# Hedgehog attention plus shifted MLP: wv loaded ahead of x tiles 2 and 3, and the later jobs in a new order

## The chip, the cores and the metric

The kernel runs on one NeuronCore of a Trainium2 chip. Its time is the device time of one execution in microseconds; the figure compared is the median of several executions. The five engines are called TensorE (PE, with its weight loads PEld), VectorE (DVE), ScalarE (ACT), GpSimd (POOL) and SyncE (SP). SP computes nothing here: it issues nearly all the DMAs, one after the other.

## The reference

Input x is 2048 tokens of 448 features (bf16). It is normalised once, and two branches and x itself are summed.

```python
xn = layernorm(x)
# A: linear attention, 16 heads of 28
q, k, v = split(xn @ wqkv)
phi(t) = concat(softmax(t @ w_phi), softmax(-(t @ w_phi)))     # per head
kv, z  = phi(k)^T v, sum of phi(k) over the tokens
A      = (phi(q) kv / (phi(q) z + 1e-6)) @ wo
# B: mixer with four groups of 112 columns, shifted by +1, -1, +2, -2 tokens
h  = gelu(layernorm(xn) @ w1);  x1 = xn + shift(h) @ w2
B  = x1 + gelu(layernorm(x1) @ w3) @ w4
out = x + A + B
```

## The kernel before

The tokens are 16 tiles of 128, called by number. The weights of q and k are multiplied into `w_phi` on the chip first (the **folds**: `wpq`, `wpk`), so that one product gives what the softmax needs. The contraction over 448 is cut into halves of 64 rows; TensorE runs a matmul of the lower 64 rows and one of the upper 64 at the same time, if they write different PSUM banks and stand next to each other in its order. There are 8 PSUM banks.

Every instruction is recorded in the order in which the code calls it, and `solve` adds the semaphore waits that the data need. Each engine then runs its own instructions in the recorded order, so **the order in the code is each engine's order**, SP's too: an instruction that waits holds all that stand behind it on its engine. A buffer or bank can only be written again when its readers are done.

The program has three parts.

1. The loads, by SP and by ScalarE's queue: x tiles 0 to 5 one by one (`load_x`), `wv` and `w1` in halves (`load_half`), the other x tiles in groups.
2. `chain([...], 600, 1)`, a list of jobs written by hand. `L` is steps of the first norm of one tile: `m` statistics (VectorE), `v` the second half of them for tile 1, whose sums ScalarE makes, `r` the power -1/2 (POOL), `a` apply on VectorE, `p` apply on POOL. `XT` transposes a normalised tile on TensorE and drains it to `xnT` by the engine named; `XD` does it with a DMA transpose on SP instead. `ZV` is V of a tile (`wv`), drained by `EV`; `ZW` a tile of the w1 product, drained through gelu by `EW`; `ZR` the rest of it; `FO` a fold, drained on VectorE; `HF` the first products of k, w2 and q. A `zip` job emits its lower halves at once and queues its upper halves, which are emitted between the lower halves of later jobs. `inside(n, job, inner)` puts `inner` behind n of the job's matmuls. `do` calls what is not TensorE's: `load_w2`, `load_w4`, `load_lap(w3)`, `load_wT` (the transposed q and k weights), `rest_T` and `h_shift` (DMAs that transpose the rest of h and shift h by tokens; both on SP), `late_3` (POOL memsets), `phi_blocks`, `kv_picks`, `kv_ones`, `spin` (matmuls without use that keep TensorE busy). `vb`, `gb`, `fb` and `wb` give the PSUM banks of `ZV`, `ZW`, `FO` and of the w2 pairs.
3. `play([...])`, the steady part, again a list in order. `k0`/`k1`, `q0`/`q1`, `w0`/`w1_` are the two halves of a pair of tiles of k, q and w2; behind k1 and q1 stand two ScalarE exponentials (`k_exp`, `q_exp`), behind `w1_` two VectorE adds. `kn` (VectorE) and `kx` (POOL) normalise phi(k); `K` adds a tile to kv; `T` is SP's DMA transpose of a q tile from `eq` to `eqT`; `lo`, `sc`, `A`, `G` are the second norm of a tile (statistics, scale, apply on VectorE if the tile is in `on_dve`, else on POOL; DMA transpose of the result); `a`/`b` the halves of a pair of w3 products, drained through gelu on ScalarE; `kc`, `kb` build the attention's kv blocks; `N` is the attention of a tile; `f` 1 to 4 the last products of a pair of tiles (w4 and wo); `S` stores a tile; `wo_in` loads `wo` into `wv`.

`q_exp` of tiles i and i+1 writes slots i % 8 and i % 8 + 1 of `eq`, which has eight slots:

```python
R.act(eq[:, i % 8:i % 8 + 2, s, :, 0:DH], two(2 * b)[:, :, 0:D]...)   # q_exp
R.dma_t(eqT(i), eq_rows[:, i % 8, :])                                  # T
```

Lines in the profile: matmuls are L204, TensorE transposes L208, ScalarE's activations L212, most of VectorE and POOL L216, DMA transposes L219, other DMAs L222. Tile names are those of the memory region: `banks` is PSUM, `hi` holds `eq` and the transposed weights, `phik` later holds gelu(w3), `vaug` later the attention's and the output's buffers, `w` stands for w1, w2, w3 and w4.

## Time and profile before

| | us |
|---|---|
| median of 3 runs | 174.32 (174.0 to 176.05) |
| the profiled execution's own time | 174.06 |
| its span | 172.3 |
| TensorE matmul busy | 166.9 (97%) |
| VectorE busy | 110.9 (64%) |
| POOL busy | 90.0 (52%) |
| ScalarE busy | 82.0 (48%) |

The span goes from the first to the last instruction of the program; the time of the execution is 1.8 us longer. All times of views are counted from the span's start. A busy TensorE is one with a matmul in flight; as matmuls overlap, short waits between them don't show as idle. SP and the queues of other engines (SPq, ACTq) are shown by what they issue; the time from the start of an issue to the landing of the data is a column of its own.

### The profile page before, as it was taken

To read this page: it belongs to the slowest core of one execution; us is meant where nothing else is said; L and a number is where in the kernel's file an instruction comes from. 1 tells how busy PE (TensorE), PEld (TensorE's weight loads), DVE (VectorE), ACT (ScalarE), POOL (GpSimd) and SP (SyncE) were. 2 spreads that over 40 slices of the span, in tenths; PEclk is the share of its full clock that TensorE was granted. 3 is DMA by queue.
4 is the path that set the end of the run, shared out by engine and by line. 5 is a ranking of instruction groups with operands and counts; after the bars stand their busy time and mean duration, and the time that the engine had idled before them with its cause. 6 is when DMAs were issued, how large, how long until landed. Compare 5 with 4: busy or idle time off the path is not lost.

```text
span 172.3 us, 5315 instructions
## 1 busy us (share of the span) xinstructions
PE 166.9 (97%) x2308; PEld 96.6 (56%) x2308; DVE 110.9 (64%) x251; ACT 82.0 (48%) x107; POOL 90.0 (52%) x121
## 2 busy tenths in 40 slices
PE   7799999999999999999999999999999999999994
PEld 7545888874555555554544554554545545555563
DVE  3799943749999989918955873525817416474621
ACT  4478876777987899646133322133133212044000
POOL 5456970004779999860574289332441522724540
PEclk9999999999999999999999999999999999999999
DMA  5995546499998955161057557554961120233331
GB/s 127 330 248 92 104 67 158 87 352 220 334 159 174 135 124 138 21 76 30 11 114 97 111 105 146 94 103 106 136 135 34 30 57 4 57 34 84 88 87 50
DMA packets 51111, 20.07 MB, mean 116 GB/s; under 512 B 42256, under 2 KB 50384, under 8 KB 51088
## 3 DMA queue, kind: packets, MB, share of 16 engines
q1 hardware_dynamic: 49968, 18.86, 56.0%
q10 hardware_dynamic: 1120, 0.87, 1.6%
q8 instruction: 18, 0.29, 0.8%
q14 instruction: 5, 0.04, 0.1%
HBM read 7.14 MB, written 1.84 MB: 52 GB/s over the span
## 4 chain that ended last, share of the span: by engine, by line
PE 92%; DMA 3%; ACT 1%; DVE 1%; issue 0%; ACTq 0%
PE banks L204 91%; DMA wv<-in_A_wqkv_dram 3%; PE banks L208 1%; ACT xnT L212 1%; DVE wpq L216 1%; ACT vaug L212 0%; ACTq L222 0%; ACT L366 0%; DVE vaug L216 0%
## 5 line engine op out<-in xcount | busy, mean ns | idle before, releaser
L212 ACT ACTIVATE phik<-banks 128x1024 bf16<-128x1024 f32 (+1 forms) x44 | 42.2, 986 | 63.6 <-PE banks L204 63.4
L204 PE MATMUL banks<-gT,w 64*128 64x512 bf16 x392 | 49.2, 376 | 0.1
L216 DVE TENSOR_TENSOR vaug<-banks,vaug 128x464 f32<-128x464 f32 (+3 forms) x65 | 32.8, 513 | 20.6 <-PE banks L204 18.9
L204 PE MATMUL banks<-w,phik 64*128 64x448 bf16 (+3 forms) x434 | 45.2, 343 | 0.0
L216 POOL TENSOR_TENSOR xnT<-vaug 128x196 bf16<-128x196 f32 (+1 forms) x32 | 18.1, 587 | 47.8 <-DVE vaug L216 47.8
L204 PE MATMUL banks<-wv,xnT 64*128 64x448 bf16 (+3 forms) x222 | 32.8, 346 | 1.4 <-DMA wv<-in_A_wqkv_dram 1.2
L204 PEld LDWEIGHTS banks<-w,phik 64*128 64x128 bf16 (+1 forms) x434 | 22.9, 94 | 19.4 <-issue 0.4
L722 POOL TENSOR_TENSOR phik<-phik,rks 128x1792 bf16<-128x1792 bf16 x8 | 25.6, 3214 | 10.7 <-DVE rks L216 10.5
L204 PEld LDWEIGHTS banks<-gT,w 64*128 64x128 bf16 x392 | 18.0, 94 | 18.7 <-PE banks L204 1.1
L204 PEld LDWEIGHTS banks<-wv,xnT 64*128 64x128 bf16 (+1 forms) x222 | 13.8, 94 | 10.0 <-ACT xnT L212 1.6
L216 POOL TENSOR_TENSOR vaug<-xn,xtok 128x448 f32<-128x448 bf16 x16 | 16.2, 1033 | 0.2 <-DVE vaug L216 0.2
L216 DVE TENSOR_REDUCE ksum<-phik 128x64 f32<-128x1792 bf16 x8 | 16.0, 1994 | 0.0
L216 POOL TENSOR_TENSOR rs<-mv,mhalf 128x1 f32<-128x1 f32 (+2 forms) x18 | 12.4, 694 | 6.6 <-DVE mv L216 6.6
L204 PE MATMUL banks<-xnT,w 64*128 64x512 bf16 x84 | 15.7, 377 | 0.0
L216 DVE RECIPROCAL vaug<-banks 128x16 f32<-128x16 f32 x16 | 4.0, 252 | 17.4 <-PE banks L204 17.4
L204 PE MATMUL banks<-wpk,xnT 64*128 64x448 bf16 x112 | 14.9, 350 | 0.1
L212 ACT ACTIVATE hi<-banks 128x896 bf16<-128x896 f32 x16 | 13.8, 931 | 1.0 <-PE banks L204 1.0
L204 PE MATMUL banks<-wpq,xnT 64*128 64x448 bf16 x112 | 14.2, 349 | 0.0
L204 PE MATMUL banks<-w,hT 64*128 64x448 bf16 x96 | 12.9, 349 | 0.0
L216 DVE TENSOR_TENSOR xn<-banks,xn 128x512 bf16<-128x512 f32 (+1 forms) x16 | 9.0, 606 | 3.0 <-PE banks L204 2.9
L216 DVE BATCH_NORM_STATS2 st<-xn 128x6 f32<-128x448 bf16 x16 | 9.4, 589 | 0.0
L216 DVE BATCH_NORM_STATS2 st<-xtok 128x6 f32<-128x448 bf16 x15 | 9.1, 606 | 0.0
(72 smaller groups left out, 165.4 us busy)
## 6 DMA issues: line engine op xcount, KB each, us to landing
w<-in_B_w_dram SPq DMA_DIRECT2D x2, 896.0 KB, 5.7
out_dram<-vaug SPq DMA_DIRECT2D x15, 112.0 KB, 2.0
w<-in_B_w_dram SPq DMA_DIRECT2D x1, 1568.0 KB, 10.0
xtok<-in_A_x_dram SPq DMA_DIRECT2D x2, 448.0 KB, 7.4
wv<-in_A_wo_dram SPq DMA_DIRECT2D x2, 224.0 KB, 2.9
xtok<-in_A_x_dram SPq DMA_DIRECT2D x3, 112.0 KB, 2.6
xtok<-in_A_x_dram ACTq DMA_DIRECT2D x3, 112.0 KB, 2.8
w<-in_B_w_dram SPq DMA_DIRECT2D x1, 336.0 KB, 4.3
```

The lines of the kernel that those rows point to most:

```text
L204: self.op("PE", lambda e: e.matmul(out, lhsT, rhs, start=start, stop=stop, skip_group_check=True), [out], [lhsT, rhs], tile=self._tile(lhsT))
L208: self.op("PE", lambda e: e.transpose(out, in_, ident), [out], [in_, ident], tile=self._tile(in_))
L212: self.op("ACT", lambda e: e.activation(out, in_, func, **kw), [out], [in_] + aps)
L216: self.op(eng, lambda e: getattr(e, name)(out, *args, **kw), [out], aps)
L722: R.op(pool, lambda e: e.tensor_tensor(ph, ph, wide, op=ALU.mult), [ph], [ph, wide, *after])
```

## The change

`wv` is issued second on both queues, ahead of x tiles 2 and 3, and the halves of `wv` and `w1` trade queues. The first norm's steps are put in an order in which tiles 2 and 3 come after tile 1's sums and the spins ahead of the first transpose; one power instruction still serves tiles 1 and 2. All later jobs of the chain stand in a new order, with other banks and in part other engines for the drains. The DMAs that the chain issues move with it: `load_w2` comes ahead of the DMA transposes of tiles 8, 11 and 9 (it came behind), `load_w4` ahead of `w3`, `rest_T(1)` and `h_shift(1)` (it came last). In the play list the same 258 jobs stand in a new order; among them T goes 0, 2, 3, 5, 1, 4, 7, 6, 8, 12, 10, 11, 9, 14, 13, 15, and nine tiles instead of five have their second norm applied on VectorE. The number of instructions is the same but for the drains and applies that change engine.

```diff
         R.op("ACT", lambda e: e.preload_act_table_set("gelu_apprx_tanh_and_others"), [], [])
         load_x(0, 1)
         load_x(1, 1, "ACT")
+        load_half(wv, wv_d, 0)
+        load_half(wv, wv_d, 1, "ACT")
         load_x(2, 1)
         load_x(3, 1, "ACT")
-        load_half(wv, wv_d, 1)
-        load_half(wv, wv_d, 0, "ACT")
         load_x(4, 1)
         load_x(5, 1, "ACT")
-        load_half(w1, B_w1, 1)
-        load_half(w1, B_w1, 0, "ACT")
+        load_half(w1, B_w1, 0)
+        load_half(w1, B_w1, 1, "ACT")
         load_x(6, 2)
         load_x(8, 4)
         load_x(12, 4)
...
-        fb = {(1, 0): 2, (1, 2): 2, (0, 0): 2, (0, 2): 5}
+        fb = {(1, 0): 1, (1, 2): 6, (0, 0): 0, (0, 2): 5}
...
-        wb = {0: 3, 2: 2, 4: 2, 6: 0, 8: 0, 10: 0, 12: 2, 14: 2}
+        wb = {0: 1, 2: 2, 4: 2, 6: 0, 8: 0, 10: 0, 12: 2, 14: 2}
...
-        vb = {0: 7, 1: 6, 2: 0, 3: 2, 4: 4, 5: 5, 6: 1, 7: 0, 8: 4, 9: 5, 10: 0, 11: 6, 12: 3, 13: 2, 14: 0, 15: 1}
-        gb = ((5, 2, 3), (7, 6, 5), (4, 1, 0), (7, 7, 4))
+        vb = {0: 5, 1: 4, 2: 1, 3: 2, 4: 4, 5: 5, 6: 2, 7: 1, 8: 3, 9: 6, 10: 4, 11: 3, 12: 7, 13: 0, 14: 4, 15: 7}
+        gb = ((7, 2, 3), (6, 7, 0), (5, 3, 0), (2, 1, 4))
-            L(("m", 0), ("m", 2), ("r", 0, 1), ("a", 0), ("m", 3), ("v", 1), ("r", 1, 2), ("a", 2), ("a", 1), ("r", 3, 1)),
-            XT(0, 2, 1, "ACT"), do(spin, 5, 256), L(("a", 3), ("m", 4), ("m", 5), ("r", 4, 1), ("r", 5, 1)),
-            inside(1, ZV(0, EV(0, "ACT", 1)), XT(2, 5, 1, "ACT")), XT(3, 3, 1, "ACT"), ZV(2, EV(2, "ACT", 1)),
-            inside(1, ZV(3, EV(3, "ACT", 1)), XT(1, 3, 1, "ACT")), ZV(1, EV(1, "ACT", 1)), L(("a", 4), ("m", 7)),
-            ZW(0, 0, EW(0, 0, 1)), L(("a", 5)), XT(5, 0, 1, "ACT"),
-            L(("m", 6), ("m", 9), ("r", 7, 1), ("m", 8), ("r", 6, 1), ("r", 8, 1), ("a", 7), ("a", 6), ("m", 10)), ZW(0, 2),
-            L(("m", 11), ("a", 8)), XD(8), L(("m", 12)), XT(4, 0, 1, "ACT"), L(("r", 9, 1)), ZW(0, 1, EW(0, 1, 2)), L(("a", 9)),
-            ZV(4, EV(4, "ACT", 1)), XD(9), XT(7, 0, 1, "ACT"), L(("r", 10, 2), ("a", 10)), XT(6, 6, 1, "ACT"), L(("m", 13)),
-            ZV(5, EV(5, "ACT", 1)), do(phi_blocks), ZV(7, EV(7, "DVE", 1)), ZW(1, 1, EW(1, 1, 1)), ZV(6, EV(6, "ACT", 1)),
-            L(("p", 11), ("r", 12, 1), ("m", 15)), inside(2, ZW(1, 0, EW(1, 0, 1)), XT(10, 2, 1, "ACT")), L(("r", 13, 1)),
-            ZW(1, 2, EW(1, 2, 1)), L(("p", 12), ("r", 15, 1)), inside(3, ZV(8, EV(8, "ACT", 1)), FO(1, 0, 0)), L(("m", 14)),
-            XD(11), L(("r", 14, 1)), do(load_wT, 0, (1, 2, 3)), L(("a", 13)), inside(1, ZV(10, EV(10, "ACT", 1)), FO(1, 0, 1)),
-            L(("a", 15)), ZR(0, 7, (rest_out, 0, 7), (rest_T, 0), (h_shift, 0)), ZV(9, EV(9, "DVE", 1)), XT(12, 3, 1, "ACT"),
-            L(("p", 14)), do(load_w2), XT(13, 1, 1, "ACT"), ZV(11, EV(11, "ACT", 1)), ZW(2, 2, EW(2, 2, 1)), do(late_3),
-            XT(14, 2, 2, "DVE"), ZW(2, 0, EW(2, 0, 1)), ZW(2, 1, EW(2, 1, 1)), do(load_lap, w3, B_w3), FO(1, 2, 0),
-            inside(3, ZW(3, 0, EW(3, 0, 1)), FO(1, 2, 1)), ZR(1, 6, (rest_out, 1, 6)),
-            inside(3, ZW(3, 2, EW(3, 2, 1)), FO(0, 0, 0)), ZV(15, EV(15, "ACT", 1)), do(kv_ones),
-            inside(3, ZW(3, 1, EW(3, 1, 1)), FO(0, 0, 1)), do(rest_T, 1), inside(1, ZV(14, EV(14, "ACT", 1)), FO(0, 2, 0)),
-            FO(0, 2, 1), ZV(13, EV(13, "ACT", 1)), ZV(12, EV(12, "DVE", 1)), HF(0, 0), do(kv_picks), HF(1, 0), HF(2, 0), HF(0, 1),
-            do(h_shift, 1), HF(1, 1), do(load_w4), HF(2, 1)], 600, 1)
-
-        on_dve = (4, 6, 7, 9, 12)
+            L(("m", 0), ("r", 0, 1), ("a", 0)), do(spin, 5, 256), XT(0, 2, 1, "ACT"),
+            L(("v", 1), ("m", 2), ("m", 3), ("r", 1, 2), ("a", 2)), ZV(0, EV(0, "ACT", 1)),
+            L(("a", 1), ("r", 3, 1), ("a", 3), ("m", 4)), XT(2, 0, 1, "ACT"), L(("r", 4, 1)), XT(3, 2, 1, "ACT"),
+            L(("m", 5), ("m", 6), ("p", 4), ("r", 5, 1), ("r", 6, 1), ("m", 7)), XT(1, 6, 1, "ACT"), L(("m", 8)),
+            ZV(2, EV(2, "ACT", 1)), do(load_w2), ZV(3, EV(3, "ACT", 1)), L(("a", 5)), ZV(1, EV(1, "ACT", 1)), L(("r", 8, 1)),
+            ZW(0, 0, EW(0, 0, 1)), XT(4, 0, 1, "ACT"), L(("r", 7, 1), ("m", 11), ("a", 6), ("p", 8)), ZW(0, 2),
+            inside(1, ZW(0, 1, EW(0, 1, 2)), XT(5, 5, 1, "ACT")), ZV(4, EV(4, "ACT", 1)),
+            L(("a", 7), ("m", 10), ("m", 13), ("r", 10, 2), ("m", 9), ("p", 11)), XT(7, 0, 1, "ACT"),
+            L(("m", 15), ("r", 9, 1)), XT(6, 6, 1, "ACT"), L(("r", 15, 1)), ZV(5, EV(5, "ACT", 1)), ZV(7, EV(7, "DVE", 1)),
+            L(("a", 10), ("m", 12)), ZW(1, 1, EW(1, 1, 1)), L(("a", 9)), ZV(6, EV(6, "ACT", 1)),
+            inside(2, ZW(1, 2, EW(1, 2, 1)), XT(10, 4, 1, "DVE")), L(("r", 13, 1)), ZW(1, 0, EW(1, 0, 1)), XD(8), XD(11),
+            ZV(8, EV(8, "ACT", 1)), XD(9), do(phi_blocks), FO(1, 0, 0), ZV(10, EV(10, "ACT", 1)), L(("m", 14), ("a", 15)),
+            inside(1, ZR(0, 7, (rest_out, 0, 7), (rest_T, 0), (h_shift, 0)), FO(1, 0, 1)),
+            L(("r", 14, 1), ("r", 12, 1), ("a", 14), ("a", 12)), do(load_wT, 0, (1, 2, 3)), ZV(9, EV(9, "ACT", 1)),
+            ZV(11, EV(11, "DVE", 1)), L(("p", 13)), XT(12, 4, 1, "ACT"), XT(14, 1, 2, "DVE"), ZW(2, 2, EW(2, 2, 1)),
+            inside(3, ZW(2, 0, EW(2, 0, 1)), FO(1, 2, 0)), XT(13, 1, 1, "DVE"), FO(1, 2, 1), do(load_w4),
+            ZW(2, 1, EW(2, 1, 1)), ZW(3, 2, EW(3, 2, 1)), do(late_3), inside(2, ZW(3, 0, EW(3, 0, 1)), FO(0, 0, 0)),
+            FO(0, 0, 1), FO(0, 2, 0), ZV(15, EV(15, "DVE", 1)), ZR(1, 3, (rest_out, 1, 3)), do(load_lap, w3, B_w3),
+            ZV(14, EV(14, "DVE", 1)), ZW(3, 1, EW(3, 1, 1)), HF(1, 0), ZV(13, EV(13, "DVE", 1)), FO(0, 2, 1),
+            ZV(12, EV(12, "DVE", 1)), HF(0, 0), do(rest_T, 1), HF(1, 1), do(kv_picks), HF(2, 0), HF(0, 1), do(kv_ones),
+            do(h_shift, 1), HF(2, 1)], 600, 2)
+
+        on_dve = (3, 4, 5, 10, 11, 12, 13, 14, 15)
...
-            (T, 0), (T, 1), (k0, 1), (w0, 2), (kn, 0), (k1, 1), (w1_, 2), (lo, 0), (q0, 1), (k0, 2), (kx, 0), (k1, 2), (kn, 1), (w0, 4),
-            (kx, 1), (q1, 1), (T, 2), (T, 3), (q0, 2), (lo, 1), (w1_, 4), (kn, 2), (q1, 2), (T, 4), (T, 5), (lo, 3), (k0, 3), (K, 0), (k1, 3), (kn, 3),
-            (kx, 2), (lo, 2), (kx, 3), (q0, 3), (sc, 0), (K, 1), (q1, 3), (T, 6), (T, 7), (A, 1), (A, 0), (k0, 4), (G, 0), (A, 3), (w0, 6),
-            (A, 2), (K, 2), (k1, 4), (G, 1), (G, 2), (K, 3), (G, 3), (q0, 4), (w1_, 6), (q1, 4), (k0, 5), (K, 4), (kn, 4),
-            (w0, 8), (k1, 5), (q0, 5), (kx, 4), (K, 5), (lo, 4), (w1_, 8), (kn, 5), (q1, 5), (K, 6), (k0, 6), (w0, 10),
-            (k1, 6), (kx, 5), (q0, 6), (w1_, 10), (lo, 5), (q1, 6), (k0, 7), (K, 7), (kn, 6), (k1, 7), (q0, 7), (lo, 6),
-            (K, 8), (q1, 7), (lo, 7), (w0, 12), (kn, 7), (wo_in,), (kx, 6), (a, 0), (sc, 4), (w1_, 12), (b, 0), (A, 4),
-            (G, 4), (A, 6), (K, 9), (A, 5), (G, 5), (G, 6), (a, 1), (K, 10), (A, 7), (K, 11), (b, 1), (a, 2), (K, 12),
-            (b, 2), (kx, 7), (a, 3), (w0, 14), (a, 4), (G, 7), (lo, 9), (b, 3), (K, 13), (b, 4), (K, 14), (K, 15), (a, 5),
...
+            (q0, 1), (k0, 1), (T, 0), (w0, 2), (k1, 1), (lo, 1), (lo, 0), (kn, 0), (kx, 0), (w1_, 2), (q1, 1), (k0, 2),
+            (q0, 2), (k1, 2), (w0, 4), (T, 2), (lo, 3), (T, 3), (kn, 1), (q1, 2), (T, 5), (w1_, 4), (K, 0), (lo, 2), (k0, 3),
+            (kx, 1), (T, 1), (K, 1), (k1, 3), (T, 4), (kn, 2), (q0, 3), (sc, 0), (k0, 4), (q1, 3), (K, 3), (w0, 6), (kn, 3),
+            (k1, 4), (kx, 2), (kx, 3), (w1_, 6), (q0, 4), (kn, 4), (T, 7), (wo_in,), (K, 2), (A, 3), (T, 6), (q1, 4),
+            (k0, 5), (A, 2), (w0, 8), (A, 0), (k1, 5), (q0, 5), (w1_, 8), (lo, 5), (q1, 5), (K, 4), (G, 2), (A, 1), (kn, 5),
+            (k0, 6), (kx, 4), (w0, 10), (k1, 6), (q0, 6), (w1_, 10), (lo, 6), (lo, 4), (G, 1), (kx, 5), (lo, 7), (q1, 6),
+            (K, 5), (G, 0), (T, 8), (K, 6), (k0, 7), (sc, 4), (q0, 7), (k1, 7), (K, 8), (G, 3), (w0, 12), (q1, 7), (kn, 6),
+            (w1_, 12), (A, 4), (lo, 11), (A, 5), (a, 0), (lo, 9), (K, 10), (kn, 7), (K, 7), (b, 0), (lo, 10), (K, 11),
+            (G, 5), (a, 1), (w0, 14), (a, 2), (kx, 6), (A, 7), (b, 1), (b, 2), (K, 12), (A, 6), (w1_, 14), (a, 3), (G, 4),
...
```

## The prediction

> **What bounds the kernel now.** I read the page's busy shares, then its chain, then busy time by stage, the timeline of TensorE at the head, and last the timeline of SP's queue, which the change rearranges most.
>
> ```profile
> PE 166.9 (97%) x2308; PEld 96.6 (56%) x2308; DVE 110.9 (64%) x251; ACT 82.0 (48%) x107; POOL 90.0 (52%) x121
> PE banks L204 91%; DMA wv<-in_A_wqkv_dram 3%; PE banks L208 1%; ACT xnT L212 1%; DVE wpq L216 1%; ACT vaug L212 0%; ACTq L222 0%; ACT L366 0%; DVE vaug L216 0%
> ```
>
> TensorE is the chain: 91% of the span is one matmul after another, and one DMA (`wv`) is the only other link above 1%. Columns of the next view: stretch, then busy time and instructions of each engine, clock, DMA share, GB/s.
>
> ```profile
> 5.43:7.57 2.14, 0.94 (x14) 0.61 (x14) 1.28 (x5) 0.60 (x1) 1.23 (x2) 1.00 1.05 345
> 7.57:12.40 4.83, 4.65 (x67) 2.63 (x68) 4.66 (x14) 3.33 (x7) 2.41 (x4) 1.00 1.20 296
> 12.40:37.30 24.90, 24.81 (x448) 19.49 (x446) 15.35 (x41) 18.55 (x32) 10.17 (x17) 1.00 0.63 126
> 37.30:66.20 28.90, 28.80 (x423) 15.47 (x420) 27.89 (x39) 25.05 (x31) 22.84 (x12) 1.00 1.06 197
> 66.20:170.00 103.80, 103.52 (x1330) 54.39 (x1326) 58.81 (x149) 31.58 (x33) 50.40 (x66) 1.00 0.41 79
> ```
>
> From 12.4 us on TensorE is never idle for long; from 37.3 to 66.2 us VectorE is just as full (27.89 of 28.90) and the DMA engines are full too (1.06). A busy TensorE hides waits, so I went through the starts of its matmuls: a pair of half-height 448-column matmuls takes 0.187 us, and every larger distance is a stall. After 13 us these add up to only 1.9 us; 0.75 us of them lie after 56 us. So a new order of the later jobs can win 1.9 us at the very most, and lose without limit. What else can be won lies ahead of 13 us.
>
> **The head.** The next rows are TensorE's, from its timeline.
>
> ```profile
> 5.43 0.29 PE L208 MATMUL banks<-ident,xn 64*128 64x64 bf16 x8
> 5.65 0.72 PE L204 MATMUL banks<-gT 128*128 128x256 bf16 x5
> 7.57 0.35 PE L204 MATMUL banks<-wv,xnT 64*128 64x448 bf16 x1 [1.20 <-DMA wv<-in_A_wqkv_dram]
> 10.62 0.74 PE L204 MATMUL banks<-wv,xnT 64*128 64x448 bf16 x6 [0.17 <-ACT xnT L212]
> ```
>
> Tile 0 is transposed at 5.43, and then TensorE waits for `wv` until 7.57. The landings, issue plus time to landing: x2 3.86, x3 4.05, `wv` 6.47 (SP) and 7.43 (ACT), x4 7.62, x5 8.06. The change lets `wv` trade places with x2 and x3. The same bytes go through the same queues, so what is ahead of x4 ends when it did. `wv` took 2.6 us behind its predecessor on SP and 3.4 us on ACT; behind x0 (3.25) and x1 (3.42) it lands at 5.85 and 6.8, a gain of 0.6 us. x2 then takes the time that x4 took behind `wv` (1.15 us on SP, 0.6 on ACT): 7.0 and 7.4, a loss of 3.1 to 3.4 us. Bounds for x2: 6.45 (0.6 us behind `wv`) and 7.6.
>
> VectorE follows by its rows: statistics 0.62 + 0.20, step 0.77; apply 0.41; POOL's power 0.6. Tile 2's statistics 7.05-7.85, then tile 3's until 8.6 (they stand ahead of the apply), apply of 2 to 9.0, of 1 to 9.4, of 3 to 9.8. Tile 1 waits too: its power is now one instruction with tile 2's. Before, all four were normalised by 8.09. TensorE does tile 0's transposes (five spins now ahead of them, +0.5), four `wv` matmuls, and is idle until 9.0; the transposes of tiles 2, 3, 1 end at 10.4. By 10.4 us the kernel before has issued 17 `wv` matmuls and 32 transposes, 2.0 us of work; the new one 4 and 32, 0.8 us. It is **1.2 us behind**. From there it has all it needs, while the old one loses another 0.5 us until 14 us; so 0.7 us behind at 15 us (bounds 0 and 1.5, the two landings of x2 and whether ScalarE, 3.3 of 4 us busy here, keeps up).
>
> **From 15 to 37 us.** Per job nothing is added: the same 16 V products, 12 w1 tiles, folds and 13 TensorE transposes. Drains move from ScalarE to VectorE (V of tiles 11, 13, 14, 15; transposes of 10 and 13: 0.62 or 0.37 us each), which has room (15.35 of 24.90). On SP the three `w2` loads (24.39 to 26.95 before) now stand ahead of the transposes of tiles 8, 11, 9. SP issued without a pause from 7.5 to 34 us, so these three go from 15.65 to about 17.4, and the last, which also needs tile 9's apply at about 20.5, lands at 23.5 where V of tile 9 is due at 23: 0 to 1 us. The fold drain ahead of the first k product keeps about its 0.3 us stall. Bank by bank the new numbers leave each drain (0.54 to 1.09 us) at least one job, so I take the banks at nothing (bounds -0.6, all this stage's stalls, and +1). Together the delay at 37 us is 0.5 to 1.5 us.
>
> **The transposes of eq, which I think decide.** SP's queue:
>
> ```profile
> 28.31 4.55 SPq L222 DMA_DIRECT2D hT<-hT  x6
> 32.90 1.14 SPq L222 DMA_DIRECT2D w<-in_B_w_dram  x2
> 34.08 1.29 SPq L219 DMA_TRANSPOSE hRT<-gT  x1
> 35.41 3.85 SPq L222 DMA_DIRECT2D hT<-hT  x6
> 39.30 0.59 SPq L222 DMA_DIRECT2D w<-in_B_w_dram  x1
> 40.02 18.45 SPq L219 DMA_TRANSPOSE eqT_lo<-hi  x8
> ```
>
> The loads are w3 (32.90) and w4 (39.30). The first transpose T(0) spent 6.74 us in its issue, until 46.76, w4's last bytes; the first lands at 50.16, the second, T(1), at 53.33, the fifth at 56.21. `eq` has eight slots: q_exp of pair 4 writes slots 0 and 1 and must wait for T(0) and T(1).
>
> ```profile
> 53.62 1.73 ACT L212 ACTIVATE hi<-banks 128x896 bf16<-128x896 f32 x2 [0.39 <-PE banks L204]
> ```
>
> That is this q_exp, released by TensorE: T(1) was done 0.3 us earlier. The new order makes T(1) the fifth (T 0, 2, 3, 5, 1), and puts w4 and w3 both ahead of the shift of h, which is ahead of T(0). Work on SP ahead of w4 is what was ahead of w3, so w4 issues at about 33; its bytes (5.3 us before, 42 to 47.3) go from 35 to 40.3, w3's (34 to 39.5) to 45.6, rest and shift (2.6 us) to 48. T(0) leaves its issue at 47.3, half a us later than before, and by the old cadence the fifth lands 9.4 us later: 56.7. q_exp takes 1.75: 58.5. The next q product of pair 5, (q0, 5), uses the banks that it drains. Summed by their rows (0.755 for the first half of a k, q or w pair, 0.567 for the second, 0.226 for a KV tile) the play list has 17.5 us of TensorE work ahead of (q0, 5); the old kernel had done that much at 55.7. So it resumes **2.8 us late**. Behind the q_exp on ScalarE stand k_exp 5 and q_exp 5, whose banks are wanted 2.1 us after. This delay is against the clock, not added to the head's: the later of the two holds, and the 0.7 us is swallowed. Bounds: T(1) at 54.3 (behind 48, five transposes of 1.0 us without pauses and 1.3 to land) gives 0.6, at 58.7 gives 4.8.
>
> The Trainium skill ("DMA: Bandwidth & Descriptors", section "Queues, rings and completion order") says that an engine's descriptors are consumed in ring order; by this rule alone, bytes in order and nothing else, T(1) would land at 54.3 and the sum be 175.0. T(0)'s 6.74 us issue agrees with the order, but the gaps of 1 to 3 us between later landings are more than bytes.
>
> **After 56 us.** The wait gives VectorE and POOL 2 us to catch up, so close margins (K 14 behind the eighth k product, the first w3 products behind the fourth g transpose, both within 0.5 us by the sums) hold. Four more g_apply on VectorE (0.41 against 0.76 on POOL) lie where VectorE is half idle. The same 0.75 us of stalls: 0 (bounds -0.7 and +1).
>
> **Sum.** The profiled execution took 174.06 (span 172.3 and 1.8 around it), 0.3 below the median of 174.32. 174.06 + 2.8 + 0 = **176.9 us**.
>
> **Rivals.** (1) *T(1) in time*: transposes without pauses, 54.3; then the head's 0.7 us and 0.2 for tile 9 remain, 175.0. For it: DMA engines can move a 256 KB transpose in 1 us (49 to 51 us, 246 GB/s). Against: 135 and 24 GB/s at 47-49 and 51-53, behind the same w4. (2) *The other side: faster.* `wv` at 5.85 frees TensorE, and x2 lands with it: it needs tile 2 applied by 7.5, that is x2 by about 5.9, then the 0.6 us of the wait and half of the stalls until 13 us go, and T(1) has to be in time: -1.2 us, 172.9. For it: the DMA engines were nearly empty from 3.5 to 4.75 us, and a shorter first queue might fill this. Against: in the old order nothing behind `wv` landed before 7.6. That the change doesn't do what it says, `wv` still at 7.4, would be rival 1 or the forecast plus nothing, as T(1) holds anyway. (3) *SP held by the norms*: the transposes of 8, 11, 9 wait for POOL's and VectorE's applies with everything behind them; if w4 leaves at 35 instead of 33, T(1) lands at 58.7, +4.8: 178.9, and the first w3 products wait for the fourth g transpose.
>
> **Numbers.** Forecast 0.46 (own range 175.7 to 178.0), rival 1 0.17, rival 2 0.14, rival 3 0.23. The range 173.0 to 179.8 leaves out half of rival 2 and a quarter of rival 3. Over 2% (3.5 us, about what a measurement of this kernel can tell from no change; its runs went from 174.0 to 176.05) means below 170.8 or above 177.8. Above: most of rival 3 and an eighth of the forecast, 0.28; below: 0.03; within: 0.69.
>
> **What would show it.** Right: `wv` landing near 5.9 and 6.8, x2 near 7.0; TensorE idle from 7.6 to 9.0; T(1) landing at 56 to 57.5; ScalarE's q_exp of pair 4 released by a DMA, and TensorE idle for over 1.5 us near 56. Wrong: T(1) landing before 54; x2 before 6; a stall of over 1 us anywhere after 60, or SP waiting for a norm by over 1 us.

## The result, and the profile after

The changed kernel took **176.45 us** (median of 16 executions, 175.59 to 177.88) where the kernel before took 174.05 (16 executions on the same chip, 173.8 to 176.05): ratio 1.0136, 95% interval 1.011 to 1.0161. The forecast was 176.9. A ratio, here and below, leaves out the executions that fell in the chip's slower state, so it need not be the quotient of two medians. The profiled execution of after took 176.26 (span 174.5), that of before 174.06: 2.2 us to explain.

The page of after, its engines and the second line of its chain:

```profile
PE 165.7 (95%) x2308; PEld 99.9 (57%) x2308; DVE 118.8 (68%) x259; ACT 79.2 (45%) x102; POOL 87.7 (50%) x119
PE banks L204 68%; DVE st L216 5%; DVE ksum L216 3%; DVE xn L216 3%; DMA xnT<-xn 2%; DMA eqT_lo<-hi 2%; DMA xtok<-in_A_x_dram 2%; POOL phik L722 2%; DVE mv L216 2%; DVE g_tok L216 2%; POOL rs L216 1%; ACT hi L212 1%; ACT phik L212 1%; DVE rks L216 1%; DVE vaug L216 1%
```

TensorE's matmuls are 68% of the chain instead of 91%. VectorE, two DMA transposes and a product of POOL (`phik`, L722) are links now, none of them a large one: the loss is in several places. The same stretches of time as before (columns: stretch, then busy time and instructions of PE, PEld, DVE, ACT, POOL, clock, DMA share, GB/s):

```profile
5.43:7.57 2.14, 1.15 (x12) 0.39 (x12) 1.78 (x5) 0.60 (x1) 0.99 (x2) 1.00 1.04 349
7.57:12.40 4.83, 4.27 (x67) 2.52 (x69) 4.66 (x15) 3.68 (x7) 3.10 (x7) 1.00 1.15 259
12.40:37.30 24.90, 23.03 (x430) 17.51 (x428) 19.32 (x40) 14.88 (x26) 10.49 (x18) 1.00 0.75 134
37.30:66.20 28.90, 28.62 (x410) 17.25 (x407) 28.11 (x47) 24.14 (x29) 21.88 (x11) 1.00 1.00 203
66.20:170.00 103.80, 102.39 (x1334) 56.46 (x1331) 62.22 (x147) 32.96 (x35) 48.29 (x63) 1.00 0.41 72
```

From 12.4 to 37.3 us TensorE is idle for 1.9 us where it was for 0.1, and after 66.2 us for 1.4 instead of 0.3. VectorE carries 4 us more from 12.4 to 37.3 and 3.4 more behind 66.2. A second measure says when this shows: add up the columns of all matmuls but the spins in the order of the program, and ask how much later after reaches the sum that before has reached.

| time in before, us | 13.8 | 19.0 | 22.2 | 34.0 | 46.8 | 54.9 | 57.0 | 67.4 | 75.5 | 77.5 | 92.5 | 168.5 |
|---|---|---|---|---|---|---|---|---|---|---|---|---|
| after is later by, us | -0.69 | -0.66 | +1.63 | +1.24 | +0.67 | +1.00 | +1.23 | +1.75 | +1.64 | +2.84 | +2.18 | +2.26 |

The head gains 0.7; 2.3 us are lost at 19 to 22 us; 1 us comes back until 47 us, of which 0.7 are stalls that only the old list has (at 31.0, 38.0 and 41.7 us); then 0.2 us are lost at 56, 0.5 at 67 and 1.2 at 78 us; and some 0.5 come back, for two stalls of the old list at 79.6 and 86.1. The timeline of TensorE in after has a row behind each wait, with the releaser in brackets:

```profile
6.34 0.93 PE L204 MATMUL banks<-wv,xnT 64*128 64x448 bf16 x4 [0.69 <-ACT xnT L212]
7.77 0.29 PE L208 MATMUL banks<-ident,xn 64*128 64x64 bf16 x8 [0.50 <-DVE xn L216]
8.42 0.41 PE L208 MATMUL banks<-ident,xn 64*128 64x64 bf16 x16 [0.36 <-DVE xn L216]
...
23.41 0.54 PE L204 MATMUL banks<-wv,xnT 64*128 64x448 bf16 x3 [1.63 <-DMA xnT<-xn]
...
56.92 0.55 PE L204 MATMUL banks<-wpq,xnT 64*128 64x448 bf16 x4 [0.27 <-ACT hi L212]
...
68.25 1.04 PE L204 MATMUL banks<-gT,w 64*128 64x512 bf16 x8 [0.41 <-DMA gT<-g_tok]
...
79.67 0.63 PE L204 MATMUL banks<-vaug,phik 64*128 64x59 bf16 x32 [1.00 <-POOL phik L722]
```

These are V of tile 9 (its DMA transpose landed at 23.27), the first half of q of pair 5, the first w3 product (the fourth g transpose landed at 67.90) and K 14. By the distances of the starts they cost 1.79, 0.43, 0.54 and 1.16 us; V of tile 8 costs another 0.41 at 18.4.

SP's queue in after, the rows behind these (start and time in issue):

```profile
14.42 1.85 SPq L222 DMA_DIRECT2D w<-in_B_w_dram  x3
16.31 4.03 SPq L219 DMA_TRANSPOSE xnT<-xn  x3
...
31.57 3.10 SPq L222 DMA_DIRECT2D w<-in_B_w_dram  x3
34.71 1.98 SPq L219 DMA_TRANSPOSE hRT<-gT  x1
36.74 3.76 SPq L222 DMA_DIRECT2D hT<-hT  x6
41.63 14.02 SPq L219 DMA_TRANSPOSE eqT_lo<-hi  x7
```

w2 at 14.42 stands ahead of the transposes of tiles 8, 11 and 9, as the diff says. T(0) issues at 41.63 and is out of its issue after 1.89 us; the fifth, T(1), landed at 55.04. The q_exp of pair 4 on ScalarE is released by it:

```profile
55.14 1.73 ACT L212 ACTIVATE hi<-banks 128x896 bf16<-128x896 f32 x2 [0.94 <-DMA eqT_lo<-hi]
```

**A long instruction on POOL holds the apply on VectorE.** This was nowhere in the prediction. VectorE in after:

```profile
21.92 2.60 DVE L216 TENSOR_SCALAR xn<-xtok,mv,rs 128x512 bf16<-128x512 bf16 x2
...
69.49 2.52 DVE L216 TENSOR_SCALAR g_tok<-xn,mv,rs 128x512 bf16<-128x512 bf16 x1
...
72.70 0.37 DVE L216 TENSOR_SCALAR g_tok<-xn,mv,rs 128x512 bf16<-128x512 bf16 x1
```

and POOL in after:

```profile
22.57 1.81 POOL L434 MEMSET phik<- 128x2048 bf16 x1 [0.20 <-DVE xn L216]
...
68.65 3.21 POOL L722 TENSOR_TENSOR phik<-phik,rks 128x1792 bf16<-128x1792 bf16 x1 [0.47 <-DVE rks L216]
71.85 1.69 POOL L216 TENSOR_SCALAR g_tok<-xn,rs 128x512 bf16<-128x512 bf16 x2
76.40 3.21 POOL L722 TENSOR_TENSOR phik<-phik,rks 128x1792 bf16<-128x1792 bf16 x1 [2.85 <-DVE rks L216]
```

The same apply takes 0.37 us at 72.70 and 2.52 at 69.49. The long one ends at 72.01, 0.15 us behind POOL's product (71.86); the pair at 21.92, tiles 14 and 12, ends at 24.52, 0.14 behind the memset (24.38). The memset is released by tile 14's apply, so it starts just in time to hold tile 12's. The long apply at 69.49, tile 4's second norm, stands ahead of the eighth k norm on VectorE; that ends at 76.3, the eighth k product on POOL at 79.6, and K 14 waits for it.

So there are three suspects to be parted: w2 ahead of the transposes, T(1) as the fifth, and the applies beside POOL. The head, which came out with the other sign, is a fourth question.

### The profile page after: what moved, and what is told of

It reads as the page before. It is cut to its first block, busy times and chain, and to the rows that moved or that the text cites. A ratio compares the mean times of both kernels' runs of the same rounds, so it can differ in the third digit from the quotient of the medians.

```text
span 174.5 us, 5320 instructions
## 1 busy us (share of the span) xinstructions
PE 165.7 (95%) x2308; PEld 99.9 (57%) x2308; DVE 118.8 (68%) x259; ACT 79.2 (45%) x102; POOL 87.7 (50%) x119
## 4 chain that ended last, share of the span: by engine, by line
PE 68%; DVE 16%; DMA 7%; POOL 3%; ACT 2%; issue 1%; SPq 1%; ACTq 0%
PE banks L204 68%; DVE st L216 5%; DVE ksum L216 3%; DVE xn L216 3%; DMA xnT<-xn 2%; DMA eqT_lo<-hi 2%; DMA xtok<-in_A_x_dram 2%; POOL phik L722 2%; DVE mv L216 2%; DVE g_tok L216 2%; POOL rs L216 1%; ACT hi L212 1%; ACT phik L212 1%; DVE rks L216 1%; DVE vaug L216 1%
## 5 line engine op out<-in xcount | busy, mean ns | idle before, releaser
L204 PE MATMUL banks<-gT,w 64*128 64x512 bf16 x392 | 48.5, 376 | 0.4 <-DMA gT<-g_tok 0.4
L204 PEld LDWEIGHTS banks<-w,phik 64*128 64x128 bf16 (+1 forms) x434 | 24.1, 94 | 18.1 <-issue 0.4
L722 POOL TENSOR_TENSOR phik<-phik,rks 128x1792 bf16<-128x1792 bf16 x8 | 25.6, 3214 | 13.2 <-DVE rks L216 13.2
L204 PEld LDWEIGHTS banks<-gT,w 64*128 64x128 bf16 x392 | 19.5, 94 | 17.6 <-ACT phik L212 1.6
L212 ACT ACTIVATE hi<-banks 128x896 bf16<-128x896 f32 x16 | 13.8, 922 | 2.0 <-PE banks L204 1.1
L204 PE MATMUL banks<-w,hT 64*128 64x448 bf16 x96 | 13.4, 349 | 0.0
L212 ACT ACTIVATE hT<-banks 128x512 bf16<-128x512 f32 (+1 forms) x11 | 7.0, 638 | 4.5 <-PE banks L204 4.4
```

The source lines that it names most:

```text
L204: self.op("PE", lambda e: e.matmul(out, lhsT, rhs, start=start, stop=stop, skip_group_check=True), [out], [lhsT, rhs], tile=self._tile(lhsT))
L212: self.op("ACT", lambda e: e.activation(out, in_, func, **kw), [out], [in_] + aps)
L722: R.op(pool, lambda e: e.tensor_tensor(ph, ph, wide, op=ALU.mult), [ph], [ph, wide, *after])
```

## The experiments

Each time is a median, each ratio is to the kernel before on the same chip, with its 95% interval. Most of these intervals overlap with each other and with that of after (1.011 to 1.0161), so what one edit does is read in the traces; by their times alone only `order_4` and `order_5` are told from after.

**1. w2 behind the transposes** (`w2_late`).

```diff
-            ZV(2, EV(2, "ACT", 1)), do(load_w2), ZV(3, EV(3, "ACT", 1)), ...
+            ZV(2, EV(2, "ACT", 1)), ZV(3, EV(3, "ACT", 1)), ...
-            XT(12, 4, 1, "ACT"), XT(14, 1, 2, "DVE"), ...
+            XT(12, 4, 1, "ACT"), do(load_w2), XT(14, 1, 2, "DVE"), ...
```

> Theory: the w2 loads ahead of them make the DMA transposes of tiles 8, 11 and 9 late; with w2 behind them they issue some 1.9 us sooner, tile 9's lands near 21.4 instead of 23.3, and the stalls of TensorE at 18.4 (0.4 us) and 21.6 us (1.8 us) go. But T(1) still lands near 55.0, so the stall ahead of (q0, 5) grows from 0.4 to about 1.5 us and the time falls by 0.3 us only: 176.1. Rival A: the stalls add up, the 2.2 us come off the end: 174.3. Rival B: the transposes are late through something else (the norms of tile 9, slow packets at 20 to 21.5 us): the stall at 21.6 stays over 1 us, 176.4.

177.53 us, ratio 1.0189 (1.0128 to 1.0249): none of the three numbers. The transposes of tiles 8 and 9 landed at 17.16 and 20.88 (19.00 and 23.27 in after), both stalls were gone, and TensorE was 0.37 us ahead of the kernel before at 22 us: rival B falls. Then it lost more than it had won, in two new places, on its timeline:

```profile
24.41 0.52 PE L208 MATMUL banks<-ident,xn 64*128 64x64 bf16 x24 [1.52 <-DVE xn L216]
...
33.60 0.35 PE L204 MATMUL banks<-w,hT 64*128 64x448 bf16 x1 [1.22 <-DMA w<-in_B_w_dram]
```

The first is tile 12's apply, 2.64 us for the pair with tile 14: a wait that lay hidden behind the late transpose in after. The second is w2 itself, landed at 34.98: the new list uses it at 32 us. That is what the early w2 buys.

**2. The apply of tile 4 moved** (`a4_first`).

```diff
-... (q1, 7), (kn, 6), (w1_, 12), (A, 4), (lo, 11), (A, 5), ...
+... (q1, 7), (A, 4), (kn, 6), (w1_, 12), (lo, 11), (A, 5), ...
```

> Only (A, 4) is moved, ahead of (kn, 6) on VectorE, where no product of POOL runs beside it. Theory: its 2.52 us (0.41 elsewhere) are a wait for POOL's k product that runs beside it; moved, it takes about 0.4 us, the eighth k norm ends some 1.7 us sooner, the eighth k product ends before 78 us instead of 79.6, and the 1.2 us stall ahead of K 14 goes: 175.3. Rival: VectorE has too much ahead of the eighth k norm in any case (statistics of 11 and 9, A 5), or A(4) is slow wherever it stands: the stall stays at 0.8 us or more, 176.2 to 176.5.

177.72 us, 1.0206 (1.0142 to 1.027). VectorE:

```profile
21.98 3.78 DVE L216 TENSOR_SCALAR xn<-xtok,mv,rs 128x512 bf16<-128x512 bf16 x2
...
69.29 0.41 DVE L216 TENSOR_SCALAR g_tok<-xn,mv,rs 128x512 bf16<-128x512 bf16 x1 [2.26 <-POOL rs L216]
...
73.90 1.76 DVE L216 TENSOR_SCALAR g_tok<-xn,mv,rs 128x512 bf16<-128x512 bf16 x1
```

and POOL:

```profile
72.30 3.21 POOL L722 TENSOR_TENSOR phik<-phik,rks 128x1792 bf16<-128x1792 bf16 x1 [3.05 <-DVE rks L216]
```

Tile 4's apply takes 0.41 us where nothing of POOL runs beside it, as the theory says. Now the next one, tile 5's, lies beside the seventh product and takes 1.76; it ends at 75.66, 0.15 behind the product (75.51). The time still went up: VectorE waited 2.26 us for the scale (`sc`, POOL) in front of the moved apply, the seventh and eighth k norms were later by that, a w2 product waited 1.1 us at 72 us for VectorE's adds, and the stall ahead of K 14 grew to 1.78 us. The pair at 21.98 took 3.78 us: three memsets of POOL follow each other there until 25.61, and the second apply ends at 25.76.

**3. The old order of the loads** (`old_loads`).

```diff
-        load_half(wv, wv_d, 0)
-        load_half(wv, wv_d, 1, "ACT")
         load_x(2, 1)
         load_x(3, 1, "ACT")
+        load_half(wv, wv_d, 1)
+        load_half(wv, wv_d, 0, "ACT")
         load_x(4, 1)
```

> The changed kernel with x2 and x3 loaded ahead of wv again, its jobs as they are. Theory (from the two traces): the load order is what gains 0.65 us at 13 to 18 us, so this kernel waits for wv until about 7.5 us and is 0.5 to 1 us behind the changed kernel at 15 us; as T(1) decides at 56 us by the clock, at most 0.3 us of it are left at the end: 176.4 to 176.7. Rival A (the prediction's working): x2 early is worth more than wv early, this kernel is 0.5 us or more ahead at 15 us, 175.8 to 176.4. Rival B: the gain is the jobs' order and not the loads': no difference at 15 us.

177.94 us, 1.0216 (1.0148 to 1.0284). At 15 us it was 0.61 us ahead of the kernel before, just as after: rival B. The two executions aren't quite alike, since TensorE's clock came up at 3.95 us in after and at 5.63 here (see the last section); but `order_2`, with the new loads and the clock up at 5.88, was 0.5 us ahead, so the new load order gains nothing that these traces show. `wv` landed at 6.58 and 6.73, x2 at 3.97; in after `wv` at 4.63 and 4.82, x2 at 5.60. Either way tile 0's first product starts only when ScalarE has drained its transposes. Everything else on SP came about 0.6 us later (the first x in one piece of two tiles 9.21 against 8.61), and the transpose of tile 8 landed at 20.63, for a stall of 2.05 us. That the load order made it late isn't shown: in `kv_8` below, with the loads of after and the issue at 16.31 as in after, it landed at 20.24.

**4. The old play list behind the new chain** (`old_list`): `play([...])` and `on_dve` of the kernel before, all else as changed.

> The changed kernel up to the first q product (loads, norms, V, w1, folds), with the old list of later jobs and the old set of g_apply on VectorE. Theory: the new list costs 1.4 us (from +0.8 at 40 us to +2.2 at the end), and the old one with w4 and w3 early would have T(1) second and land it by 52: 174.9, with TensorE some 0.8 us behind the kernel before at 40 us and 0.5 to 0.9 at the end. Rival: the 0.8 us at 40 us are caught up by stalls that the old list has anyway (0.75 us): 174.2. Rival: the old list with the new SP order has a stall of its own: 176 or more.

176.07 us, 1.0109 (1.0075 to 1.0143). T(1), second here, landed at 50.49, and no matmul waits for it. TensorE is 1.9 us behind at 24 us and 2.0 at the end. That is the last rival's number, but hardly its reason: the one stall of the old list that is longer behind the new chain takes 0.65 us at 39.6 instead of 0.2 at 38.0. So in these executions the chain alone costs nearly all of it, and behind it the new list ends little later than the old one: the lag of 0.8 us that I took as the chain's at 40 us was small only because the new list has fewer stalls between 31 and 42 us.

**5. w2 where it lands in time, and the memset behind tile 12** (`order_2`), **and with T(1) second** (`order_2t`).

```diff
-    R.op(pool, lambda e: e.memset(pad, 0.0), [pad], [xn[:, NT - 2, :]])
+    R.op(pool, lambda e: e.memset(pad, 0.0), [pad], [xn[:, NT - 4, :]])
-            ZV(2, EV(2, "ACT", 1)), do(load_w2), ZV(3, ...
+            ZV(2, EV(2, "ACT", 1)), ZV(3, ...
-            ... do(load_wT, 0, (1, 2, 3)), ZV(9, EV(9, "ACT", 1)),
+            ... do(load_wT, 0, (1, 2, 3)), do(load_w2), ZV(9, EV(9, "ACT", 1)),
```

> Two edits: w2 behind the last weight transposes (issued near 23 us, so that it lands well ahead of its first use at 31 us), and POOL's memset of phik's pad waits for tile 12's apply (the last on VectorE) instead of tile 14's. Theory: VectorE's two applies near 21.9 us take 0.7 us together instead of 2.6 (and 3.8 in a4_first), since no memset of POOL runs beside the second; the transposes of tiles 8 and 9 land by 17.2 and 21; so the stalls at 18.4, 21.6 and 22.5 to 24.8 us all go, and TensorE is within 0.3 us of the kernel before at 30 us. From there: T(1) lands as in all runs of this list at 55.0 to 56.0, so TensorE waits 1.3 to 2.3 us ahead of (q0, 5) and the end stays near 176.0 to 176.6 (the two delays are not added). Rival A: they are added; T(1) comes in time, 174.2 to 174.8. Rival B: the long applies have nothing to do with the memset: 2.6 us again and a stall of over 1 us at 22 to 25 us.

> order_2, and T(1) second instead of fifth. Theory: T(1) lands near 50.5, as in old_list, nothing waits ahead of (q0, 5), and the gain of order_2 reaches 66 us: TensorE within 0.5 us of the kernel before there; left are 0.4 us at 67 and 1.2 us at 78 us (K 14), less the 0.7 us that the kernel before loses at 79 to 86: 174.6. Rival: T(1) was not what held order_2, no difference from it.

`order_2`: 177.39 us, 1.0165 (1.0097 to 1.0233). `order_2t`: 176.59, 1.012 (1.0075 to 1.0165). The two applies took 1.11 and 0.73 us together instead of 2.60: rival B falls, it is the memset. VectorE of `order_2`:

```profile
21.65 1.11 DVE L216 TENSOR_SCALAR xn<-xtok,mv,rs 128x512 bf16<-128x512 bf16 x2
```

Its second apply still waits for an apply on POOL, which ends at 22.61, 0.14 us ahead of it. The stall at 24 us was gone in both. But w2 now stood ahead of the shift of h on SP, whose last part landed at 35.34 and 34.65 (33.37 in after) and held the first w2 product for 1.3 and 0.9 us; and SP had to wait for the norms of tiles 11 and 9 (0.8 and 0.4 us), a wait that w2 had filled. Tile 9's transpose, issued at 18.34 and 18.40, landed at 22.62 in `order_2`, for a stall of 1.3 us, and at 20.79 in `order_2t`, for none. What T(1) does is seen in the two timelines of TensorE, `order_2` first:

```profile
58.65 0.55 PE L204 MATMUL banks<-wpq,xnT 64*128 64x448 bf16 x4 [0.89 <-ACT hi L212]
```

```profile
56.91 0.92 PE L204 MATMUL banks<-wpq,xnT 64*128 64x448 bf16 x8
```

A wait of 1.05 us by the starts with T(1) fifth (it landed at 56.77, so rival A falls too), none with T(1) second. `order_2t` was 1.0 us behind at 15 us in its profiled execution, of which more below.

**6. The eighth k norm and product first** (`kv_8`).

```diff
-        on_dve = (3, 4, 5, 10, 11, 12, 13, 14, 15)
+        on_dve = (3, 10, 11, 12, 13, 14, 15)
-            (w1_, 12), (A, 4), (lo, 11), (A, 5), (a, 0), (lo, 9), (K, 10), (kn, 7), (K, 7), ...
+            (w1_, 12), (kn, 7), (lo, 11), (a, 0), (lo, 9), (K, 10), (K, 7), ...
-            ... (kx, 6), (A, 7), (b, 1), ... (kx, 7), (a, 4), ...
+            ... (kx, 6), (kx, 7), (A, 5), (A, 4), (A, 7), (b, 1), ... (a, 4), ...
```

> The changed kernel with the eighth k norm right behind the seventh on VectorE, the eighth k product right behind the seventh on POOL, and the g_apply of 4 and 5 on POOL behind both. Theory: nothing of VectorE stands beside a product that it would have to wait for; the eighth k norm ends by 72.5 instead of 76.3, the eighth product by 76 instead of 79.6, and the stall of 1.2 us ahead of K 14 goes: 1.1 us faster than the changed kernel on the same chip. Rival: POOL has no room for the two g_apply (0.78 us each), and the w3 products of the second group wait for its g transposes near 88 us by 1 us or more: no gain.

176.39 us, 1.0125 (1.0069 to 1.0181); the interval is too wide for a difference of 1 us from after. In the trace the eighth norm ended at 73.0, the eighth product at 76.32, and K 14 waited for nothing. 0.73 us were lost again at 86 us, where the w3 products of the second group waited for their last g transpose (86.79), behind T(12) on SP: the theory, with a part of the rival.

**7. All of these** (`order_3`), with the fourth g transpose ahead of T(8); and **the same with w2 put between** the transposes of tile 8 and of tiles 9 and 11, and the last g transposes of the second group moved up (`order_4`).

```diff
-            ... ZW(1, 0, EW(1, 0, 1)), XD(8), XD(11), ZV(8, EV(8, "ACT", 1)), XD(9), do(phi_blocks), ...
+            ... ZW(1, 0, EW(1, 0, 1)), XD(8), do(load_w2), XD(9), XD(11), ZV(8, EV(8, "ACT", 1)), do(phi_blocks), ...
-            ... (a, 3), (G, 5), (G, 4), ... (K, 9), (G, 7), ... (G, 6), (a, 5), ...
+            ... (a, 3), (G, 5), (G, 4), (G, 7), (G, 6), ... (K, 9), ... (a, 5), ...
```

> All of it: order_2, T(1) second, the edits of kv_8, and the fourth g transpose ahead of T(8). Theory: each of the causes found is gone, so stalls after 15 us add up to less than 1 us, and the time is that of the kernel before, less the 0.7 us of its own stalls at 79 to 86 us: 173.2 to 174.0. Rival: a cause is missing from the list; over 174.5.

> The changed kernel with w2 between the DMA transpose of tile 8 and those of 9 and 11 (where SP waits for tile 9's and 11's norms anyway, so that the shift of h is not pushed back as in order_2 and order_3), 9 ahead of 11, POOL's memset behind tile 12's apply, T(1) second, the fourth g transpose ahead of T(8), the edits of kv_8, and the last g transposes of the second group ahead of T(12)'s successors, where kv_8 had lost 0.7 us. Theory: the transpose of tile 9 leaves SP at 18.1 instead of 18.9 us and lands near 22, 0.5 us of stall; nothing at 24, 33, 57, 78 and 86 us; TensorE within 0.3 us of the kernel before from 30 us on: 173.6 to 174.4. Rival: transposes behind the bytes of w2 land no sooner wherever they are issued (23.3), and the 1.8 us stall stays: 175.0 to 175.6.

`order_3`: 176.0 us, 1.0105 (1.0071 to 1.0139), by the rival: it has `order_2`'s wait for the shift of h, `kv_8`'s at 86 us, and one of 1.0 us for tile 9's transpose (landed at 22.46). `order_4`: **174.58 us**, 1.0023 (0.9999 to 1.0046), a little over the theory's range. Of the changed kernel's five stalls after 15 us one is left, and one of 0.2 us for the shift of h at 34.2 us is new; VectorE of `order_4` shows the pair of applies, and its TensorE the transpose of tile 9, landed at 22.92:

```profile
21.88 0.83 DVE L216 TENSOR_SCALAR xn<-xtok,mv,rs 128x512 bf16<-128x512 bf16 x2
```

```profile
23.05 0.54 PE L204 MATMUL banks<-wv,xnT 64*128 64x448 bf16 x3 [1.31 <-DMA xnT<-xn]
```

**8. The head alone on the kernel before** (`new_head`), and **the loads alone** (`new_head_loads`). The loads are those of the change in both; in the first, the jobs up to V of tile 1 are too, in the old banks.

```diff
-            L(("m", 0), ("m", 2), ("r", 0, 1), ("a", 0), ("m", 3), ("v", 1), ("r", 1, 2), ("a", 2), ("a", 1), ("r", 3, 1)),
-            XT(0, 2, 1, "ACT"), do(spin, 5, 256), L(("a", 3), ("m", 4), ("m", 5), ("r", 4, 1), ("r", 5, 1)),
...
+            L(("m", 0), ("r", 0, 1), ("a", 0)), do(spin, 5, 256), XT(0, 2, 1, "ACT"),
+            L(("v", 1), ("m", 2), ("m", 3), ("r", 1, 2), ("a", 2)), ZV(0, EV(0, "ACT", 1)),
+            L(("a", 1), ("r", 3, 1), ("a", 3), ("m", 4)), XT(2, 5, 1, "ACT"), L(("r", 4, 1)), XT(3, 3, 1, "ACT"),
...
```

> The kernel before with only the head of the change: wv ahead of x2 and x3, and the norms and the first four transposes and V products in the new order; all from the fifth tile on as before. Theory from the traces: TensorE is 0.1 to 0.7 us ahead of the kernel before at 15 us (the runs with the new head so far: 0.65, 0.37, 0.10, 0.29, 0.65 ahead, one 1.0 behind), and the list behind it keeps most of that: 173.7. Rival (the prediction's first step): x2 late costs more than wv early wins, 0.7 us behind at 15 us and 174.0 to 174.8. Rival: the gain is swallowed by a later wait by the clock: 174.05.

> The kernel before with only the loads exchanged, wv ahead of x2 and x3, and every job in the old order. Theory (from old_loads, which was as far at 15 us with the old loads): which of the two comes first makes less than 0.3 us at 15 us, since the same bytes are in by 7.5 us either way; 173.8 to 174.3. Rival: the statistics of tiles 2 and 3 stand ahead of the first applies on VectorE in the old order, so x2 at 5.6 us holds tile 0's apply too: 0.5 to 1.5 us behind at 15 us, 174.6 to 175.5.

176.41 us, 1.0087 (1.0052 to 1.0122), and 176.21, 1.0105 (1.0071 to 1.0139). At 15 us they are 1.83 and 2.18 us behind, and exactly as much at the end. The list behind them is that of the kernel before, and it neither gives back nor takes anything. The loads alone show the wait of their rival: tile 0's transposes come 1.5 us late, at 6.83, behind VectorE's statistics of tile 2. The rest, and most of what `new_head` lost, was in neither theory. Stretches of `new_head` (columns as above; the clock is third from the end):

```profile
8.00:9.00 1.00, 0.53 (x15) 0.33 (x12) 0.97 (x4) 0.68 (x2) 0.00 (x0) 1.00 1.06 360
9.00:10.00 1.00, 0.54 (x10) 0.35 (x12) 0.96 (x4) 0.51 (x2) 0.81 (x2) 0.62 1.10 363
10.00:11.00 1.00, 1.00 (x7) 0.45 (x4) 0.97 (x4) 0.50 (x1) 0.56 (x2) 0.50 1.98 206
11.00:12.00 1.00, 1.00 (x7) 0.78 (x7) 0.97 (x4) 0.54 (x1) 0.56 (x2) 0.50 1.13 150
12.00:13.00 1.00, 1.00 (x10) 0.58 (x7) 0.97 (x3) 0.14 (x1) 0.48 (x1) 0.67 2.31 11
```

TensorE's granted clock falls to 0.50 at 9.2 us and comes back at 12.7. The shares of the clock that are missing, (0.38 + 0.50 + 0.50 + 0.33) x 2, make 3.42 us at half speed; each pair of `wv` matmuls takes 0.37 instead of 0.19. `new_head_loads`, `order_2t` and `order_5` below have the same 3.42 us; no other profile here has any. In `new_head` three executions had a mean clock of 1.00, at 174.23, 174.33 and 174.98, and all others (below 1.00) took 175.85 or more. So without the dip this head, as built here, is worth nothing to the old list, and with it costs about 2 us. A part of this is my own, and no run takes it away: I had given tile 1's transposes the banks of tile 3's, for a wait of 1.1 us at 8.3 us, just ahead of the dip.

**9. Tile 9 transposed by TensorE, and the w2 product later** (`order_5`): on top of `order_4`.

```diff
-            ... inside(2, ZW(1, 2, EW(1, 2, 1)), XT(10, 4, 1, "DVE")), ... XD(8), do(load_w2), XD(9), XD(11), ...
+            ... inside(2, ZW(1, 2, EW(1, 2, 1)), XT(9, 4, 2, "DVE")), ... XD(8), XD(11), do(load_w2), ...
-            ... ZW(3, 1, EW(3, 1, 1)), HF(1, 0), ZV(13, ...), FO(0, 2, 1), ZV(12, ...), HF(0, 0), ...
+            ... ZW(3, 1, EW(3, 1, 1)), ZV(13, ...), FO(0, 2, 1), ZV(12, ...), HF(0, 0), HF(1, 0), ...
```

> order_4 (174.21 in its profiled execution, of which 1.3 us are the wait of V of tile 9 for its DMA transpose, landed 22.9, at 21.6 us), with tile 9 transposed by TensorE together with tile 10, so that only tiles 8 and 11 go through SP; w2 behind these two; and the first half of the first w2 product moved behind the first half of the first k product, since the shift of h lands at 34.2 us whatever TensorE does and would otherwise take back what is won. Theory: TensorE loses 0.2 us to eight more transposes and wins the 1.3 us, nothing else between 12 and 66 us is late by more than 0.3 us: 173.1 to 173.5, ahead of the kernel before. Rival A: V of tile 11 then waits for its transpose as tile 9 did (landing after 22.6 instead of before 21): 174.0 to 174.5. Rival B: the w2 product, moved, starts VectorE's work behind it 2.5 us later, and VectorE is full from 37 to 66 us: a new wait of 0.5 us or more ahead of a KV product before 66 us, 173.8 to 174.6.

174.21 us (173.04 to 175.09), 1.0001 (0.9977 to 1.0025). The profiled execution is one with the dip of the clock: 1.88 us behind at 11.6 us, of which it wins back half, and 0.9 behind at the end. After 12 us its only stall over 0.15 us is one of 0.2 at 36 us; neither rival shows. Of its twelve executions those at a mean clock of 1.00 took 173.04 to 174.34, the five below 1.00 174.37 to 175.09. So the changed kernel with these mends is level with the kernel before; the median of the seven without the dip is 173.77, 0.3 us under the kernel before's 174.05. These seven were picked after the fact, so that is a hint and not a result. The head of the kernel before with this tail was not run.

## Why the prediction was right or wrong

**The number was right by luck; its parts were not right.** 176.9 was 2.8 us from T(1) and nothing else. T(1)'s term was too large by about 1.6 us, and what comes after 56 us, put at nothing, cost 1.0. Measured are, in the same order: head -0.7, 15 to 37 us +1.9 (to +1.2 at 34 us), 37 to 55 us -0.2, T(1) +0.2, after 56 us +1.0 net.

*Head, "1.2 us behind at 10.4, 0.7 behind at 15 us": wrong in sign for this execution.* The step that failed is that "what is ahead of x4 ends when it did". It ended sooner: x4 landed at 6.28, not 7.62, `wv` at 4.63 and 4.82 (forecast 5.85 and 6.8), x2 at 5.60 (7.0, bounds 6.45 to 7.6). From 3.5 to 4.75 us the DMA engines moved 362 GB/s instead of 143; rival 2 had named this (as nearly empty engines), and its condition, x2 by about 5.9, was met. What I had put on the loads is not theirs, though: `old_loads` was as far at 15 us. And the 0.7 us hang on when the clock comes up, 3.95 us in after's profiled execution: the others with this head were 0.65 to 0.10 us ahead without the dip, the less the later it came up (0.1 at 6.99), and 1.0 to 1.8 us behind with the dip. TensorE's idle time was there, but at 5.5 (0.86 us), 6.9 (0.67) and 7.9 (0.52), not from 7.6 to 9.0.

*15 to 37 us, "0 to 1 us": too small, measured 2.2 us at the two transposes.* The landing came out (tile 9's at 23.5, measured 23.27), but by luck: its apply was done at 18.18, not 20.5, and the transpose, issued at 18.94, took 4.3 us to land (3.4 in before). The need didn't come out: V of tile 9 was due at 21.6, because the head was ahead, not behind. The drains put on VectorE were called free since it "has room (15.35 of 24.90)". The share hid that one apply would stand beside a memset of POOL; `w2_late` showed that this alone costs 1.7 us as soon as the transpose is in time. Two waits of about the same length lay on top of each other.

*T(1), "2.8 us late": the mechanism was right (`order_2` against `order_2t`), the size was not.* q_exp of pair 4 was released by T(1) after a wait of 0.94 us, and TensorE lost 0.43, a sixth of the forecast. The mis-sized term is T(1)'s landing: 55.04, between the lower bound (54.3) and the forecast (56.7), since w4 issued at 31.57, not 33, and T(0) was out of its issue at 43.5 and not 47.3, ahead of w3's landing (43.91). That T(0)'s issue lasts until the last bytes ahead of it was a misreading of before, too: 46.76 was called w4's last bytes, and w4 landed at 49.25. Rival 1 had the better landing, and the Trainium skill ("DMA: Bandwidth & Descriptors", section "Queues, rings and completion order") with its 54.3 too. The first transposes do land in the order of the bytes (T(0) at 49.24, behind the last shift of h at 48.57); the gap from 51.39 to 54.13 between the third and the fourth is not explained by that. (By its own terms the lower bound is 54.3 + 1.75 - 55.7, 0.4 us and not 0.6.)

The rule that the later of two delays holds, and not their sum, is borne out. T(1)'s landing plus 1.75 less 55.7 gives 1.1 us in after, and TensorE was 1.3 us late at that product; in `w2_late`, `a4_first`, `old_loads`, `kv_8` and `order_2` it gives 2.0, 2.0, 2.0, 2.0 and 2.8 us, and TensorE was 2.2, 2.2, 2.1, 2.2 and 3.0 us late.

*After 56 us, "close margins hold": wrong, +1.0.* Both margins that I had named were passed: the first w3 product waited 0.54 us for the fourth g transpose (T(8) had been put ahead of it on SP), and K 14 1.16 us for the eighth k product. "Four more g_apply on VectorE (0.41 against 0.76 on POOL) lie where VectorE is half idle" is the step: one of them took 2.52.

*Banks at nothing*: no wait of TensorE for a drain in after but those of the head and of q_exp. Right.

*Rival 3, SP held by the norms*: not in after, SP issued steadily until 40.5 us; but in `order_2`, as soon as w2 no longer filled the wait.

## What to carry to other kernels

An apply on VectorE is only as cheap as its row if no long instruction of POOL runs beside it: before work is moved between the two engines, lay their timelines side by side, and look for the long POOL instructions that fall on it. A wait seen in a trace may cover another of the same length, so an edit that removes the first is judged by where the next one appears, not by the time alone. In a hand-made order loads that look early may fill a wait of their queue and feed something later: `w2_late` gave back more than it had won.
